# Fused top-k attention and mixture of experts: the first expert slot's gather goes ahead of its weights and one turn sooner

## The chip, the core and the metric

One NeuronCore of a Trainium2 chip runs the whole program. The metric is the device time of one execution in microseconds (us); the number given is the median of several executions. A profile is one execution of its own, with its own time.

## What is computed

The input is 8 batches of 8 heads with 576 positions of 64 numbers. Attention keeps, in every row of 576 scores, those that are at least the 32nd largest, and its output (4608 tokens of 512 numbers) goes through a mixture of 8 experts, of which each token uses one:

```python
scores = scale * np.matmul(q, k.transpose(0, 1, 3, 2))
kth = np.partition(scores, -32, axis=-1)[..., -32:-31]
attn = softmax(np.where(scores >= kth, scores, -1e9))
x = (attn @ v).transpose(0, 2, 1, 3).reshape(4608, 512)
logits = x @ w_gate + modality_bias[modality_id]
e_idx = np.argmax(logits, axis=1)
out[mask] = gate_w[mask, None] * (np.maximum(x[mask] @ w1[e], 0.0) @ w2[e])   # for each expert e
```

## The kernel before

The attention is cut into 288 tiles of 128 x 576 scores, 36 for a batch and 9 for a pair of heads. The main loop has one turn `i` for a tile, and every turn writes down one stage of some ten tiles: the scores of tile i+2 (`qk`, L384, copied to SBUF by ScalarE in `sevac`, L389), the search for the 32nd largest of tile i on VectorE (`subs`, `chain`, `find`, L396 to L438), the sign pass on ScalarE (`sign`, L428) and the product with it on GpSimd (`pool_y`, L434), the exponential, and the transposes of tile i-9 (`trans`, L492). `sign` of a turn writes one of two buffers K, so it waits for the `pool_y` of the turn before; `find` of a turn reads the y that the turn before wrote. In the first 48 tiles two of three use another path for the mask (`hide`, `hidden`, `masked`, L465 to L477), which gives GpSimd a second pass (L471).

When a batch is done its tokens are routed (`route`) and scattered by five indirect DMAs of GpSimd (`send`, L611) into a table `xs` in DRAM, sorted by expert. Expert work comes in slots of 256 rows of one expert. A slot picks its expert on VectorE (`sched`: `pick` and `done`, L677 to L693), reads the choice into a register of SyncE (`which`, L697), gathers its rows (`rows`, `xg<-xs`, L701), loads the expert's weights in four pieces each (`load_w1`, L722, and `load_w2`, L727), takes the token numbers (`tokens`, L713 to L716), turns the rows over on TensorE (`xt`, L769) and multiplies (`hid`, L796, and `outp`, L809). All these loads and the attention's own (`load`, L140 to L147, the V of a pair at the turns with j = 7) are issued by SyncE, in the order in which the program writes them.

What stands where is decided when the program is written, by lists and a ledger:

- `rush` holds the steps of a slot's start. A turn takes up to 18 of them and stops at a `PAUSE`, which it uses up. `sent` empties what is left of the scatters (`sends`); otherwise a turn sends two at its end. `go` lets the slot's products begin in the next turn.
- Weights wait in `wl`, from which a turn issues one piece at its end (none where j is 3 or 4); a product that needs a piece takes it out at once (`loaded`).
- The ledger `spare_pe` gains `STEP` = 3.4 a turn (1.0 from turn 294), loses the `COST` of the attention's products in this turn, gains 0.1 for each small step on VectorE and is capped at `CAP` = 2.6. As long as it is above zero, pieces of expert work are written into the turn: 0.22 for a quarter of `xt`, 0.88 for half an `hid` or one `outp`. After a block's last product the next block starts in the next turn at the earliest. Where no expert work is at hand, six bfloat16 products keep TensorE busy instead (`keep_warm`, L969).
- The main loop's last turn is 309. What is left of the expert work then follows, and six further slots are run one by one (`slot`, L1065 and L1081), after their rows and weights have been split in two parts by ScalarE and VectorE (`turn_rows`, L1036; `parts`, L1020 and L1021). `in_advance` writes the first of these splits among the leftovers.

The first slot starts at turn 50. Its list before the change is

```python
rush.extend(pick + [begin] + l1[:2] + done + [PAUSE, sent] + rows + [PAUSE, PAUSE] + go + [l1[2], l1[3], PAUSE] + tok)
```

where `pick` has ten entries, `done` five, and `l1` are the four pieces of w1.

Of the kernel before, what the change touches and what calls it, by code (L numbers as in the profile page):

```python
# [77 lines left out]
def kernel(  # L78
# [43 lines left out]
    PAUSE = lambda: None  # L122

    def load(p, what, b=None, queues={}):

        o = LD.setdefault(p, {})
        h0 = 2 * (p % HP)
        for nm in what:
            Q = queues.get(nm, SP)
            src = {"k": k, "q": q, "v": v}[nm]  # L130
            g = src[p // HP] if b is None else src[ds(b, 1)].rearrange("o h s d -> (o h) s d")
            if nm == "v":
                t = vtail[p % 2]
            else:
                if nm == "k":
                    o["kq"] = ld.tile([128, 2, D], FT, name="kqt", bufs=1)
                t = o["kq"][0:64] if nm == "k" else o["kq"][64:128]
            m = ld.tile([128, 2, 4, D] if nm == "v" else [128, 4, 2, D], FT, name=nm + "m", bufs=2 if nm == "v" else 1)
            if nm == "v":
                Q.dma_start(m.rearrange("p h c d -> p h (c d)"),  # L140
                             g[h0:h0 + 2, 0:512, :].rearrange("h (p c) d -> p h (c d)", c=4))
            else:
                for h in range(2):
                    Q.dma_start(m[:, :, h, :], g[h0 + h, 0:512, :].rearrange("(p c) d -> p c d", c=4))
            Q.dma_start(t[:64, 0:3:2, :] if nm == "v" else t, g[h0:h0 + 2, 512:, :].rearrange("h p d -> p h d"))
            if nm == "v":
                Q.dma_start(t[64:, 1, :], g[h0 + 1, 512:, :])  # L147
            o[nm] = (m, t)
# [496 lines left out]
    def chores():  # L645

        while chore:
            chore.popleft()()
# [76 lines left out]
    def load_w2(s, g):  # L725
        SL[s]["w2"][g] = True
        SP.dma_start(w2b[:, 2 * g:2 * g + 2, :],  # L727
                     w2[ds(SL[s]["e"], 1), g * 256:g * 256 + 256, :].rearrange("o (c p) d -> p (o c) d", p=128))
# [129 lines left out]
    rush = deque()  # L858
    moe = deque()
    sends = deque()  # L860
# [7 lines left out]
    def ready(n, whole):  # L868
# [5 lines left out]
        for g in range(4):  # L874
            load_w2(n, g)

    plan = {"ready": -1, "go": False}
    alone = [False]
    wl = deque()

    def weight(f):

        if alone[0]:
            f()
        else:
            wl.append(f)

    def more_moe():

        n = nslot[0]  # L890
        b = seen[0] // S
        full = PB[b - 1] if b <= len(PB) else int(seen[0] / SLOT - 0.9)
        fits = lambda x: x >= PB[-1]
        if plan["ready"] == n:
            if moe or not plan["go"]:
                return
            chores()
            nslot[0] += 1
            nxt = full >= n + 2
            moe.extend(expert(n, True, nxt, fits(n + 1), True))  # L900
            if nxt:
                plan.update(ready=n + 1, go=True)
        elif full >= n + 1:
            now = SL[n - 1] if moe else {"xt": True, "used": [4, 4]}
            if not now["xt"]:
                return
            plan.update(ready=n, go=False)
            pick, rows, done, tok = sched(n, fits(n))
            free = []

            def begin():
                free.extend(now["used"])
                now["nxt"] = True

            def take(x, g):
                return lambda: weight(lambda: (load_w1, load_w2)[x](n, g)) if g < free[x] else None
            l1 = [take(0, g) for g in range(4)]
            l2 = [f for g in range(4) for f in (take(1, g), PAUSE)]
            go = [lambda: plan.update(go=True)]
            if n == 0:  # L920
                def sent():

                    while sends:
                        sends.popleft()()
                rush.extend(pick + [begin] + l1[:2] + done + [PAUSE, sent] + rows + [PAUSE, PAUSE] + go + [l1[2], l1[3], PAUSE] + tok)
            else:
                begun, rest = ([], go) if moe else (go, [])
                rush.extend(pick + [begin] + rows + rest + l1[:1] + done + [PAUSE, l1[1], l1[2], PAUSE, l1[3]] + begun + [PAUSE] + tok)
            side.extend(l2)
# [189 lines left out]
    for i in range(LAST):  # L1119
# [5 lines left out]
        p, j = divmod(i, 9)  # L1125
# [49 lines left out]
        if p + 2 < NPAIR and j in LJ:  # L1175
            load(p + 2, "kq"[LJ.index(j)])
        if j == VJ and p < NPAIR:
            load(p, "v")
        b1, r = divmod(i - (TL + 1), 36)
        if b1 > SOON:  # L1180
            b1, r = divmod(i - (TL + 2), 36)
# [53 lines left out]
        while seen[0] and spare_pe > 0:  # L1235
            if i < NT + ME and not alone[0]:
                more_moe()
            if not moe:
                break
            c, f, new = moe[0]  # L1240
            if (new() if callable(new) else new) and after:
                break
            moe.popleft()
            f()
            spare_pe -= c
# [236 lines left out]
```

## Time and profile before

| | us |
|---|---|
| median of 3 executions | 1193.09 (1192.94 to 1196.3) |
| the profiled execution | 1193.59 |
| its span, first to last instruction | 1191.9 |
| TensorE busy (matmul) | 1153.1 |
| VectorE busy | 1093.2 |
| ScalarE busy | 983.2 |
| GpSimd busy | 675.8 |

PE is TensorE's matmul, PEld its weight load, DVE VectorE, ACT ScalarE, POOL GpSimd, SP SyncE; SPq and POOLq are the queues in which SyncE and GpSimd issue. The chain of work that ended last is followed back from the last instruction, at each step to what released it. A wait for several semaphores is put down to the one that came last. A busy share of 100% is not an engine at its peak: matmuls are pipelined and their ends modelled.

### The profile page before, as it was taken

The numbers are of one execution on the slowest core, as the hardware profiler recorded it, in microseconds if no ns is written. First come the engines' busy times: TensorE is split into PE (matmuls) and PEld (weight loads), VectorE is DVE, ScalarE is ACT, GpSimd is POOL, SyncE is SP. The second block draws the span as 40 slices with busy tenths as digits, with TensorE's granted clock in tenths as the row PEclk, the third lists the DMA queues.
The fourth block names the chain that finished last, engine by engine and source line by source line (L and its number), as shares of the span: only waits on it lengthen the run. The fifth ranks groups of instructions, "written<-read, shape, count | busy, mean of one in ns | idle before, by whom it ended". The sixth has DMA issues, their size and how long they took to land.

```text
span 1191.9 us, 28040 instructions
## 1 busy us (share of the span) xinstructions
PE 1153.1 (97%) x7908; PEld 904.7 (76%) x7908; DVE 1093.2 (92%) x5474; ACT 983.2 (82%) x2015; POOL 675.8 (57%) x1256
## 2 busy tenths in 40 slices
PE   8889979999999999999999999999999999999998
PEld 6766768778786868778687877778686877589987
DVE  7999999999999999999999999999999999476762
ACT  6999979998899989998899898889899888355652
POOL 6888885655656565556556566657555665221111
PEclk9999999999999999999999999999999999999999
DMA  5663367663576467664786458654765554287750
GB/s 128 167 173 89 89 168 208 186 168 97 158 229 175 121 169 207 168 168 128 205 238 172 111 144 239 170 155 133 198 197 129 155 167 139 69 286 246 248 193 22
DMA packets 204323, 197.09 MB, mean 165 GB/s; under 512 B 104413, under 2 KB 151533, under 8 KB 204160
## 3 DMA queue, kind: packets, MB, share of 16 engines
q1 hardware_dynamic: 196880, 175.92, 53.1%
q0 software_dynamic: 6080, 19.00, 4.4%
q8 instruction: 66, 1.08, 0.4%
q14 instruction: 97, 0.79, 0.2%
q10 hardware_dynamic: 1200, 0.30, 0.1%
HBM read 118.63 MB, written 24.23 MB: 120 GB/s over the span
## 4 chain that ended last, share of the span: by engine, by line
PE 61%; DVE 27%; ACT 6%; issue 2%; POOL 2%; DMA 1%; SPq 1%; POOLq 0%; ACTq 0%; DVEq 0%
PE E L809 12%; PE E L796 10%; PE X L520 9%; PE S L384 7%; DVE cand L396 7%; PE T L492 6%; PE X L1081 5%; DVE mg L438 4%; PE X L1065 4%; DVE P L458 4%; PE E L1065 1%; DVE cand L407 1%; ACT K L428 1%; DVE cand L408 1%; ACT Ssb L389 1%
## 5 line engine op out<-in xcount | busy, mean ns | idle before, releaser
L396 DVE MAX8 cand<-Ssb 128x8 f32<-128x96 f32 x1728 | 389.4, 245 | 2.0 <-ACT Ssb L389 2.0
L434 POOL TENSOR_TENSOR y<-Ssb,K 128x576 f32<-128x576 f32 x288 | 368.2, 1278 | 20.4 <-ACT K L428 19.6
L428 ACT ACTIVATE K<-Ssb,n 128x576 bf16<-128x576 f32 x288 | 229.6, 797 | 8.1 <-POOL y L434 7.4
L384 PE MATMUL S<-ks,qs 128*128 128x288 f32 x992 | 223.4, 347 | 11.2 <-ACT Ssb L389 7.0
L389 ACT ACTIVATE Ssb<-S 128x576 f32<-128x576 f32 x284 | 187.6, 661 | 52.4 <-PE S L384 31.9
L438 DVE MAX8 mg<-y 128x8 f32<-128x576 f32 x288 | 213.3, 741 | 1.9 <-POOL y L434 1.9
L796 PE MATMUL E<-xgT,w1b 128*128 128x256 f32 x832 | 201.0, 384 | 3.5 <-ACT hT L800 2.4
L452 ACT ACTIVATE ex<-Ssb,sm 128x576 f32<-128x576 f32 x256 | 202.4, 791 | 0.0
L384 PEld LDWEIGHTS S<-ks,qs 128*128 128x128 f32 x992 | 153.1, 191 | 59.5 <-issue 28.0
L500 ACT ACTIVATE PT<-T 128x640 f32<-128x640 f32 (+1 forms) x288 | 193.3, 671 | 5.9 <-PE T L492 5.7
L809 PE MATMUL E<-w2b,hT 128*128 128x512 f32 x416 | 195.4, 596 | 0.7 <-ACT hT L800 0.4
L458 DVE SCALAR_TENSOR_TENSOR P<-Ssb,kth,ex 128x576 f32<-128x576 f32 x230 | 191.9, 835 | 3.7 <-ACT ex L452 3.0
L492 PE MATMUL T<-idf,P 128*128 128x128 f32 x1152 | 169.5, 274 | 6.9 <-ACT P L477 5.6
L796 PEld LDWEIGHTS E<-xgT,w1b 128*128 128x128 f32 x832 | 150.9, 190 | 30.4 <-ACT hT L800 9.0
L481 POOL TENSOR_SCALAR spare<-P 1x1 f32<-1x1 f32 x230 | 42.6, 185 | 202.1 <-DVE mg L407 168.7
L492 PEld LDWEIGHTS T<-idf,P 128*128 128x128 f32 x1152 | 137.4, 140 | 12.9 <-ACT P L477 9.3
L520 PE MATMUL X<-PT,vm 128*64 128x256 f32 (+1 forms) x1536 | 145.1, 331 | 0.3
L421 POOL TENSOR_SCALAR n<-mg 128x1 f32<-128x1 f32 x288 | 69.8, 242 | 93.1 <-DVE mg L409 74.7
L520 PEld LDWEIGHTS X<-PT,vm 128*64 128x64 f32 x1536 | 87.8, 137 | 44.2 <-issue 10.9
L809 PEld LDWEIGHTS E<-w2b,hT 128*128 128x128 f32 x416 | 73.0, 190 | 60.2 <-issue 55.1
L1087 POOL DMA_INDIRECT out_dram<-ot,tk x12 | 12.3, 1023 | 91.2 <-ACT ot L1086 91.2
L428 ACT ACTIVATION_READ_ACCUMULATOR K<-Ssb,n 128x1 f32 x288 | 63.5, 221 | 0.0
(223 smaller groups left out, 2152.8 us busy)
## 6 DMA issues: line engine op xcount, KB each, us to landing
w1b<-in_moe_w_dram SPq DMA_DIRECT2D x76, 512.0 KB
w2b<-in_moe_w_dram SPq DMA_DIRECT2D x76, 512.0 KB
ks<-st SPq DMA_DIRECT2D x62, 288.0 KB
ks<-st SPq DMA_DIRECT2D x62, 256.0 KB
qs<-st SPq DMA_DIRECT2D x124, 128.0 KB
xg<-xs SPq DMA_DIRECT2D x19, 516.0 KB
vm<-in_v_dram SPq DMA_DIRECT2D x32, 256.0 KB
km<-in_k_dram SPq DMA_DIRECT2D x63, 128.0 KB
```

The costliest lines, as they stand in the source:

```text
L384: PE.matmul(ps[:, hf, :288], l, m, start=(n == 0), stop=(n == len(terms) - 1))
L389: A.activation(sb.rearrange("p (a b) -> p a b", a=2), T[i]["ps"], AF.Copy, scale=0.125)
L396: return [lambda s=s: V.max(c[:, s * 8:s * 8 + 8], T[i]["S"][:, bnd[s]:bnd[s + 1]]) for s in range(NSUB)]
L428: A.activation(t["K"], t["S"], AF.Sign, scale=2.0 ** -24 - 1.0, bias=t["n"][:, 1, i % 3:i % 3 + 1], accum_out=t["n"][:, 0, i % 3:i % 3 + 1])
L434: G.tensor_tensor(t["y"], t["S"], t["K"], op=OP.mult)
L438: V.max(t["mg"][:, i % 3, 24:32], t["y"])
L452: A.activation(t["ex"], t["S"], AF.Exp, bias=t["s"][:, i % 3:i % 3 + 1])
L458: V.scalar_tensor_tensor(t["P"], t["S"], kth[:, i:i + 1], t["ex"], op0=OP.is_ge, op1=OP.mult, accum_out=dn)
L492: PE.transpose(T[i]["pt"][:, x, :], (Pm if c == 4 else Pb[c % 2])[:, h * 512 + x * 128:h * 512 + x * 128 + 128], idf)
L520: PE.matmul(o.rearrange("p (a b) -> p a b", a=2) if j < 8 else o, l, r, start=(c == 0), stop=(c == 4))
L796: PE.matmul(ps[:, f % 2], w1b[:, c, f * 128:(f + 1) * 128], xgT[:, c, :], start=(c == 0), stop=(c == KC - 1))
L809: PE.matmul(o["py"], hT[:, f, t * 128:(t + 1) * 128], w2b[:, f, :], start=(f == 0), stop=(f == FC - 1))
```

## The change

The two first pieces of w1 move from ahead of the gather to behind it, one `PAUSE` behind the gather goes and one further down is added, and a load of V that falls due while scatters are still unsent is put on a list that is emptied behind `go`.

```diff
+    held_ = deque()
     plan = {"ready": -1, "go": False}
...
             if n == 0:
+                held = [lambda: [held_.popleft()() for _ in range(len(held_))]]
+
                 def sent():
 
                     while sends:
                         sends.popleft()()
-                rush.extend(pick + [begin] + l1[:2] + done + [PAUSE, sent] + rows + [PAUSE, PAUSE] + go + [l1[2], l1[3], PAUSE] + tok)
+                rush.extend(pick + [begin] + done + [PAUSE, sent] + rows + l1[:2] + [PAUSE] + go + held + [l1[2], l1[3], PAUSE, PAUSE] + tok)
...
         if j == VJ and p < NPAIR:
-            load(p, "v")
+            if sends:
+                held_.append(lambda p=p: load(p, "v"))
+            else:
+                load(p, "v")
```

## Rows read from the trace of the kernel before

**Rows 1.** The page's parts 1 and 4: busy time, and the chain by engine.

```profile
PE 1153.1 (97%) x7908; PEld 904.7 (76%) x7908; DVE 1093.2 (92%) x5474; ACT 983.2 (82%) x2015; POOL 675.8 (57%) x1256
...
PE 61%; DVE 27%; ACT 6%; issue 2%; POOL 2%; DMA 1%; SPq 1%; POOLq 0%; ACTq 0%; DVEq 0%
```

**Rows 2.** Chain of waits, 150 to 200 us: start, length, what.

```profile
165.22 1.27 POOL ex L471
...
172.44 1.24 POOL y L434
173.71 0.75 DVE mg L438
...
189.80 2.63 PE E L796 x12
```

**Rows 3.** Timeline of POOL: start, length, line, operation, count, [idle before, releaser].

```profile
167.89 1.02 POOL L611 DMA_INDIRECT xs<-x,dest  x1 [0.16 <-issue]
...
169.21 1.00 POOL L611 DMA_INDIRECT xs<-x,dest  x1 [0.20 <-issue]
...
170.85 0.94 POOL L611 DMA_INDIRECT xs<-x,dest  x1 [0.28 <-issue]
```

**Rows 4.** Timeline of DVE, the searches of turns 52 and 53.

```profile
169.41 0.74 DVE L438 MAX8 mg<-y 128x8 f32<-128x576 f32 x1
...
173.71 0.76 DVE L438 MAX8 mg<-y 128x8 f32<-128x576 f32 x1 [1.19 <-POOL y L434]
```

**Rows 5.** Timeline of ACT, the sign pass of turn 53.

```profile
173.71 0.77 ACT L428 ACTIVATE K<-Ssb,n 128x576 bf16<-128x576 f32 x1 [3.11 <-POOL y L434]
```

**Rows 6.** Timeline of PE, turns 53 to 55.

```profile
171.34 0.82 PE L969 MATMUL E<-onesb 128*128 128x256 bf16 x6
176.19 1.33 PE L384 MATMUL S<-ks,qs 128*128 128x288 f32 x4 [4.04 <-ACT Ssb L389]
...
178.87 1.49 PE L969 MATMUL E<-onesb 128*128 128x256 bf16 x6
...
185.56 0.66 PE L769 MATMUL E<-idf,xg 128*128 128x128 f32 x4
```

**Rows 7.** Windows of 2 us: length, busy by engine, granted clock, DMA share, GB/s.

```profile
174.00:176.00 2.00, 0.00 (x0) 0.00 (x0) 2.00 (x14) 1.75 (x4) 1.99 (x3) 0.84 0.84 296
176.00:178.00 2.00, 1.79 (x6) 1.44 (x7) 2.00 (x6) 2.00 (x5) 1.84 (x3) 0.50 0.05 15
...
182.00:184.00 2.00, 2.00 (x18) 1.42 (x19) 1.97 (x15) 2.00 (x6) 0.39 (x2) 0.96 0.49 173
```

**Rows 8.** Timeline of SP's queue, the loads around the first slot's gather.

```profile
169.52 0.46 SPq L722 DMA_DIRECT2D w1b<-in_moe_w_dram  x1
170.03 0.66 SPq L140 DMA_DIRECT2D vm<-in_v_dram  x1
...
177.13 0.36 SPq L701 DMA_DIRECT2D xg<-xs  x1
```

**Rows 9.** SP queue's waits, 160 to 180 us: total, times, longest.

```profile
SPq L701 <- DMA xs<-x,dest: 3.9, 1, 3.9
```

**Rows 10.** Chain of waits at a later slot's gather.

```profile
571.77 3.57 DMA xg<-xs
```

**Rows 11.** Chain of waits at the program's end, behind the last scatter but one.

```profile
1182.02 1.02 POOL out_dram L1087
...
1183.14 4.00 issue
```

**Rows 12.** Timeline of DVE: an instruction of turn 84, one of turn 90.

```profile
279.94 0.39 DVE L582 TENSOR_TENSOR lt<-X,rd 128x128 f32<-128x128 f32 x1 [2.56 <-PE X L574]
...
306.37 0.15 DVE L677 TENSOR_TENSOR s_av<-er 128x8 f32<-128x8 f32 x1
```

**Rows 13.** Timelines of PE and of DVE behind the main loop.

```profile
1038.99 6.28 PE L809 MATMUL E<-w2b,hT 128*128 128x512 f32 x14
...
1040.70 3.50 DVE L1021 TENSOR_TENSOR w1l<-w1b,w1h 128x1024 fp32r<-128x1024 f32 x3 [1.33 <-ACT w1h L1020]
```

## The prediction

> **What bounds the kernel now.** I read the busy times first: TensorE is busy 97% of the span and VectorE 92%, and the chain that ended last runs 61% over TensorE and 27% over VectorE [rows 1]. So most of the time follows TensorE, and a change at the first slot pays only where TensorE does without waiting, or what it need not do. Then the chain of waits about the slot: from 165.22 to 173.7 us it runs over GpSimd, then over VectorE, and at 189.80 it is on TensorE [rows 2]. The reason is in GpSimd's queue: two scatters end turn 51, the fifth opens turn 52, and each keeps GpSimd about 1.3 us from start to start [rows 3]. The products y of turn 52 come only at 172.44 [rows 2]; VectorE's search of turn 53 waits 1.19 us for them [rows 4], ScalarE's sign pass 3.11 us [rows 5], and behind that pass in ScalarE's queue stands the copy that frees the scores' PSUM, so TensorE waits 4.04 us, until 176.19 [rows 6]. Behind that hole TensorE runs at half its clock: granted 0.84 in the window that ends at 176, 0.50 after it, 0.96 in the one that starts at 182 [rows 7]. The gather is issued at 177.13, after 3.9 us of waiting for the scatters [rows 8, 9], and the slot's first transposes run at 185.56 [rows 6].
>
> **The order after the change.** The old list fills its 18 places with l1[:2], so the next turn is used up by the `PAUSE` alone, and the gather stands in turn 52. The new list has 16 steps and then the `PAUSE`: `sent` and the gather stand in turn 51, `go` in 52, the first transposes in 53 and not 55. `sent` finds three scatters unsent and writes them in one row, ahead of turn 51's y; at the top of turn 52 none is left, so V is loaded at its old place, behind the gather in SyncE's queue, and the new `held` list stays empty.
>
> **GpSimd and VectorE.** The three scatters begin at 166.65, after the pass of 165.22 [rows 2], and end near 170.3 (two starts 1.3 apart, and 1.0 for the last [rows 3]). Turn 51's y is then ready at 171.7 (1.3 more, and the gap of 0.16 ahead of it); it was there before 169.41, where VectorE's search of turn 52 starts without a wait [rows 4]. That search now waits 2.3 us; the wait of 1.19 in turn 53 goes, because y of turn 52 is no later than before (GpSimd's total is the same, in one turn fewer). VectorE: +1.1 us at turn 54.
>
> **SyncE and the gather.** Before, the fifth scatter's instruction ended at 171.79 [rows 3] and the gather went out at 177.13 [rows 8]: 5.3 us, beside w1 and V, which were issued at 169.52 and 170.03, just among them [rows 8]. Without them the nearest row is the program's end, where the release comes 4.0 us behind a scatter with the engines otherwise idle, though for 128 rows and not 64 [rows 11]. So the landing costs between something below 4.0 and 5.3; I take 4.0, since two pieces of w1 and a V, 1.3 MB, no longer run beside it: 170.3 + 4.0 = 174.3, 2.8 us earlier than now. The gather lands 3.57 us after its issue at another slot [rows 10]: 177.9. It is first in its queue, so the weights behind it don't delay it. Queued behind it are V and all four pieces of w1; some 2.4 MB (four pieces of 0.52 MB, and 0.3) at the 296 GB/s of a full window [rows 7] are in by 183, while V is needed just ahead of 185.56 [rows 6] and w1 at 189.80 [rows 2]. I cost them at nothing; if they came late, TensorE would stand in front of V, and that is in the range. On the price of a landing there is a rule that speaks against the change. The Trainium skill, page "DMA: Bandwidth & Descriptors", section "Anatomy of one DMA — SWDGE (gpsimd) path", puts a fixed 2.0 us on such a DMA, most of it the receipt from memory, plus its bytes at 436 GB/s: an estimate of 2.3 us for these 64 rows of 2 KB, whatever runs beside it. By it the gather would land at 176.2 and the sum below be about 1.7 us less; the 4.0 us of the program's end don't agree with it [rows 11], nor do the 5.3.
>
> **TensorE.** In turn 53 its products now end with two transposes that need the gather, and the scores of turn 54 stand behind them. From below it is ScalarE that holds these scores, as now, or a little sooner (175.9); from above it is a gather no faster behind its scatter than now (170.3 + 5.3 + 3.57 = 179.2, and 0.9 for the transposes at half clock). With 177.9 they start at 178.5: +2.3 us against 176.19 [rows 6]. The hole is now in two parts (about 169.9 to 173.1, where y of turn 51 is late, and 174.4 to 177.9), so I expect the half clock as now, and cost it at nothing more. Gone are two groups of warming products: 0.82 us that lay ahead of the hole and cost nothing, and 1.49 us at half clock in turn 54 [rows 6]: -1.5.
>
> **Expert work that moves.** Playing the ledger on from the constants: slot 0's first products move from turn 55 to 53, slot 1's from 75 to 72, slot 2's from 94 to 91 (its tokens are there from 90 on in either case); from turn 57 on the expert work is 3.5 units ahead, from about turn 96 to the end mostly 4.4, and of the 2.2 units left behind turn 309 none remains. A unit is one us: three pieces of 0.88 take 2.63 us [rows 2]. Where TensorE bounds, this only moves work: the early turns grow by what the late ones lose. It is worth something where VectorE bounds and TensorE has room. Turns 84 to 89 last 26.4 us from one early instruction of turn 84 to one of turn 90 [rows 12], and the ledger has 23.3 us of TensorE's work in them: 3.1 us of room, into which the new order puts 1.8 units more than the old one. -1.8.
>
> **The end.** Before, 14 records (7 pieces) of `outp`, 6.28 us, run while VectorE splits three pieces of w1 for 3.50 us, up to 1044.2 [rows 13]. The ledger leaves 5 pieces (4.4 us) behind the last transposes of x, so TensorE is through with them at 1042.9 (from 1038.5, half a us ahead of the row, which followed four transposes that are then no longer there) and with the slot's eight row transposes at 1043.9. VectorE is free at 1044.2 and needs 0.6 for half the rows (3.50/3 for 1024 columns, so half of it for 512): TensorE idles until 1044.8. +0.9; the bounds are 0 and 2, if rows or weights are later.
>
> **Sum.** +2.3 - 1.5 - 1.8 + 0.9 = -0.1 us on the execution of 1193.59 us; VectorE's +1.1 lies beside TensorE's +2.3. The profiled execution is 0.5 us above the median of the runs shown, so the forecast is 1193.0 us: the stall is not removed but moved, from ScalarE's queue to the gather.
>
> **Rivals.** *The gather holds TensorE (slower).* If scatters land no sooner after their issue than now, TensorE's turn 54 starts at 180.1: +3.9. The half clock, which lasted some 6 us behind the hole [rows 7], then covers 1.3 us of transposes and products that were not in these turns, which costs as much again, and VectorE is starved, so nothing is taken up later: +3.9 + 1.3 - 1.5 + 0.9 = +4.6, 1197.6 us. It decides from a landing at about 178.9 on. For it: the 5.3 us of now. Against it: the weights did run beside those scatters. To the same side belongs that later slots meet their gathers a turn earlier (slot 2's transposes one turn after its gather, and the chain already lost 3.57 us at one of them [rows 10]). *The hole closes (faster).* If the gather lands by 175.5, TensorE starts turn 54 at 175.9 (-0.3), has no hole of 4 us and keeps its clock, which gives back half of 6 us (-3.0); the warming products cost 0.82 and save that (-0.8), and with -1.8 and +0.9 this is -5.0, 1188.0 us. For it: DMA still moved 296 GB/s in the window up to 176 [rows 7], with w1 and V in it. Against it: y of turn 51 is late whatever the gather does, and TensorE is without scores until 173.1. *The weights were not what held the scatters, but nothing else hurts:* between forecast and first rival, and inside the forecast's band.
>
> **How the numbers follow.** A measurement of this kernel can tell about 0.3%, 3.6 us, from no change. The forecast has 0.58, with its own range 1189.6 to 1196.6 (no change); the gather that holds TensorE, with the later slots' gathers, 0.21 (slower); the closed hole 0.21 (faster). The range for 8 in 10 takes in both rivals' times: 1187.5 to 1198.0.
>
> **What would show it.** Three L611 in one row from 166.6; the search of turn 52 waiting about 2.3 us for y, and none in turn 53; the gather's issue near 174.3 with all w1b and V behind it; L769 twice, in turns 53 and 54, the first waiting for `xg`; 12 fewer records of L969; fewer `outp` behind the last transposes of x. The granted clock between 174 and 184 decides between forecast and faster rival, the start of turn 54's scores (175.9, 178.5 or 180.1) between all three. The prediction is wrong if the time follows neither: if VectorE bounds the whole attention, the 4.4 us of expert work moved early would be free, and the end would come 3 to 4 us sooner with the hole unchanged.

## The result, and the profile after

| | kernel before | changed kernel |
|---|---|---|
| median of 4 executions, us | 1193.28 (1192.94 to 1196.3) | 1208.76 (1206.77 to 1209.49) |
| ratio, 95% interval | | 1.0121 [1.0105, 1.0137] |
| the profiled execution, us | 1193.59 | 1206.77 |
| its span, us | 1191.9 | 1205.1 |

The changed kernel is 1.2% slower, outside the range of the prediction. The ratios in this text are not quotients of the medians (for the changed kernel the means give 1.0121, the medians 1.0130). From line 921 on, the lines of the changed kernel are three higher (L969 is L972, L1065 is L1068).

The page's parts 1 and 4, which answer [rows 1]:

```profile
PE 1155.7 (96%) x7896; PEld 907.4 (75%) x7896; DVE 1093.9 (91%) x5474; ACT 981.3 (81%) x2015; POOL 671.4 (56%) x1256
...
PE 68%; DVE 20%; ACT 6%; issue 2%; DMA 2%; SPq 1%; POOL 0%; POOLq 0%; ACTq 0%; DVEq 0%
```

The work is the same but for 12 products of `keep_warm`, and each engine's busy time is within 5 us of before. The 13 us are idle time and half clock. To see where they arise I take VectorE's search (L438), which stands once in every turn from 5 to 292, and subtract its start in the kernel before from its start in the changed one. This **lag** is -0.3 us at turn 51, 1.2 at turn 60, 1.8 at turn 107, 8.8 at turn 113, 9.75 at turn 292 (the last search), and 13.2 at the end of the span. So there are three steps: 1.6 us at the first slot, 7.0 at turns 107 to 113, 3.5 behind the last search. In between the lag goes up and down (it is 12.0 at turn 209), with 1.5 us left of it.

**The first slot.** Timelines of POOL, DVE, PE and SP's queue in the changed kernel (start, length, line, operation, count, [idle before, releaser]), for [rows 3, 4, 6, 8]:

```profile
166.31 1.01 POOL L611 DMA_INDIRECT xs<-x,dest  x1 [0.16 <-issue]
...
168.91 0.91 POOL L611 DMA_INDIRECT xs<-x,dest  x1 [0.22 <-issue]
...
169.88 1.28 POOL L434 TENSOR_TENSOR y<-Ssb,K 128x576 f32<-128x576 f32 x1
```
```profile
171.19 0.76 DVE L438 MAX8 mg<-y 128x8 f32<-128x576 f32 x1 [2.05 <-POOL y L434]
174.23 0.75 DVE L438 MAX8 mg<-y 128x8 f32<-128x576 f32 x1
```
```profile
172.64 1.33 PE L384 MATMUL S<-ks,qs 128*128 128x288 f32 x4 [3.10 <-ACT Ssb L389]
...
176.07 1.09 PE L769 MATMUL E<-idf,xg 128*128 128x128 f32 x4 [1.03 <-DMA xg<-xs]
...
177.66 1.31 PE L384 MATMUL S<-ks,qs 128*128 128x288 f32 x4
...
180.05 3.49 PE L796 MATMUL E<-xgT,w1b 128*128 128x256 f32 x12
```
```profile
171.99 0.38 SPq L701 DMA_DIRECT2D xg<-xs  x1
172.58 0.38 SPq L722 DMA_DIRECT2D w1b<-in_moe_w_dram  x1
```

Three scatters in a row, y behind them, one search that waits and the next that doesn't, the gather ahead of the weights, the transposes held by it, the scores of the turn behind them at 177.66: the forecast order is all there. Windows of PE's clock, where 0.50 is the lower of its two levels, for [rows 7] (length, busy by engine, granted clock, DMA share, GB/s):

```profile
170.00:172.00 2.00, 0.00 (x0) 0.00 (x0) 0.81 (x3) 0.81 (x3) 1.84 (x4) 0.82 0.59 209
172.00:174.00 2.00, 1.36 (x6) 1.35 (x7) 2.00 (x15) 2.00 (x6) 1.31 (x3) 0.50 0.44 136
...
178.00:180.00 2.00, 2.00 (x11) 1.98 (x10) 1.93 (x10) 1.97 (x5) 0.71 (x1) 0.50 0.36 119
180.00:182.00 2.00, 2.00 (x8) 1.68 (x7) 1.97 (x11) 1.40 (x3) 1.92 (x3) 0.62 0.78 259
```

**The large step.** PE and SP's queue at 360 us, and the chain of waits there (start, length, what):

```profile
354.44 1.88 PE L809 MATMUL E<-w2b,hT 128*128 128x512 f32 x4
...
360.70 1.02 PE L809 MATMUL E<-w2b,hT 128*128 128x512 f32 x2
367.12 3.78 PE L809 MATMUL E<-w2b,hT 128*128 128x512 f32 x4 [5.39 <-DMA w2b<-in_moe_w_dram]
```
```profile
336.01 0.43 SPq L727 DMA_DIRECT2D w2b<-in_moe_w_dram  x1
336.69 1.87 SPq L722 DMA_DIRECT2D w1b<-in_moe_w_dram  x2
338.77 0.94 SPq L727 DMA_DIRECT2D w2b<-in_moe_w_dram  x2
...
359.69 0.43 SPq L722 DMA_DIRECT2D w1b<-in_moe_w_dram  x1
...
362.34 0.43 SPq L727 DMA_DIRECT2D w2b<-in_moe_w_dram  x1
```
```profile
362.34 4.74 DMA w2b<-in_moe_w_dram
```

An x4 here is four records of `outp`; two records make a product. The fourth piece of slot 2's w2 is issued at 362.34, 0.6 us after TensorE has run out of work, and lands 4.74 us later. Four records then take 3.78 us, with a granted clock of 0.59 from 365 to 370 us; at full clock four take 1.88 (the row of 354.44). Between the third piece (in the row of 338.77) and the fourth stand 23 us, and in front of the fourth a piece of w1 that belongs to slot 3 (359.69). In the kernel before all four left together, and slot 3's first piece followed:

```profile
333.94 2.93 SPq L727 DMA_DIRECT2D w2b<-in_moe_w_dram  x4
...
338.31 0.37 SPq L722 DMA_DIRECT2D w1b<-in_moe_w_dram  x1
```

The program's own order says why. Slot 2 starts at turn 91, not 94, and so slot 3's gather and its first w1 pieces are written sooner (the gather in turn 96, not 101); but slot 2's w2 pieces enter the list `wl` at the pace of `side`, the queue of small steps from which a turn takes a few. So two pieces of slot 3's w1 get in line ahead of three of slot 2's w2, and a third ahead of the last. A turn issues one piece, and none where j is 3 or 4 (turns 102 and 103). The last piece is taken out in turn 105, the turn that uses it; before, it left eight turns ahead of its use.

**The end.** PE and ACT behind the main loop, for [rows 13]:

```profile
1046.12 0.18 PE L602 MATMUL X<-ohb,tri 128*128 128x40 bf16 x1 [1.37 <-DVE x L554]
...
1050.76 4.46 PE L809 MATMUL E<-w2b,hT 128*128 128x512 f32 x10
...
1057.47 0.35 PE L1068 MATMUL X<-xgh,w1h 128*128 128x256 f32 x1 [1.38 <-POOL spare L537]
1058.88 0.58 PE L1068 MATMUL X<-xgl,w1h 128*128 128x256 f32 x1 [1.05 <-DVE xgl L1024]
1059.25 0.42 PE L1068 MATMUL X<-xgh,w1l 128*128 128x256 f32 x1
```
```profile
1047.13 2.00 ACT L1023 ACTIVATE w1h<-w1b 128x1024 fp32r<-128x1024 f32 x2
1055.25 0.69 ACT L819 ACTIVATE ot<-E,sgt 128x512 f32<-128x512 f32 x1 [6.12 <-PE E L809]
1055.84 1.05 ACT L1023 ACTIVATE w1h<-w1b 128x1024 fp32r<-128x1024 f32 x1
```

Ten records of `outp` (five products) stand behind the last transposes of x, as forecast; before there were sixteen (eight). But with fewer pieces left `in_advance` has written only two splits of w1 ahead of the last result copy (L819), not three. The third split stands behind that copy in ScalarE's queue (1055.84 behind 1055.25), and the copy waits 6.12 us for its products; the split of the rows comes behind both, at 1056.78. TensorE waits 1.38 and 1.05 us for those splits (the profile names a memset of GpSimd for the first wait; that ScalarE's split of the rows, which ends about then, is what it waits for is read off, not tested). It waits 1.37 earlier, for VectorE's copy of x (L554), where the kernel before runs one product of `outp` (1032.54, 1.02 us long) and waits 0.27. Then it runs at half clock (granted 0.50 from 1060 to 1062 us) for some 15 records (0.42 us long; 0.28 later on).

The lag is VectorE's, and at the last search it hides part of TensorE's: TensorE starts the last logits (L565) at 1038.67 against 1027.06, 11.6 us behind and not 9.75. So 1.9 of the 3.5 us are products that TensorE had done ahead and that VectorE's row doesn't show yet (in e5 below, where that lead is handed back at turn 286, the two lags agree within 0.1). By the starts of TensorE's later rows in both kernels, the wait at L602 adds 0.7, the way to the first row of L1068 gives back 1.3 (fewer products, less the wait of 1.38), the second wait adds 0.7 and the half clock 1.4.

### The profile page after: what moved, and what is told of

Read it like the earlier page. It is cut to its first block, busy times and chain, and to the rows that moved or that the text cites. A ratio compares the mean times of both kernels' runs of the same rounds, so it can differ in the third digit from the quotient of the medians.

```text
span 1205.1 us, 28021 instructions
## 1 busy us (share of the span) xinstructions
PE 1155.7 (96%) x7896; PEld 907.4 (75%) x7896; DVE 1093.9 (91%) x5474; ACT 981.3 (81%) x2015; POOL 671.4 (56%) x1256
## 4 chain that ended last, share of the span: by engine, by line
PE 68%; DVE 20%; ACT 6%; issue 2%; DMA 2%; SPq 1%; POOL 0%; POOLq 0%; ACTq 0%; DVEq 0%
PE E L796 13%; PE E L809 12%; PE X L520 11%; PE S L384 9%; PE T L492 7%; DVE cand L396 5%; PE X L1084 5%; PE X L1068 4%; DVE mg L438 3%; DVE P L458 3%; PE E L1068 1%; PE X L318 1%; ACT Ssb L389 1%; ACT K L428 1%; DVE hT L465 1%
## 5 line engine op out<-in xcount | busy, mean ns | idle before, releaser
L438 DVE MAX8 mg<-y 128x8 f32<-128x576 f32 x288 | 213.1, 740 | 2.7 <-POOL y L434 2.7
L809 PE MATMUL E<-w2b,hT 128*128 128x512 f32 x416 | 196.9, 601 | 5.7 <-DMA w2b<-in_moe_w_dram 5.4
L809 PEld LDWEIGHTS E<-w2b,hT 128*128 128x128 f32 x416 | 73.6, 191 | 67.7 <-issue 57.4
```

Source lines behind the costliest of these rows:

```text
L438: V.max(t["mg"][:, i % 3, 24:32], t["y"])
L809: PE.matmul(o["py"], hT[:, f, t * 128:(t + 1) * 128], w2b[:, f, :], start=(f == 0), stop=(f == FC - 1))
```

## The experiments

The theory at this point: the first slot itself is nearly free, and the loss comes from the expert work that runs three to four products ahead from then on, through one piece of w2 and through the end. Rival 1 puts it down to the new order of scatters and loads; rival 2 says that work ahead of its loads must wait somewhere, so that the piece is only where it shows first. The lags (us behind the kernel before's profiled execution, start of L438; the end is the span's):

| run | median, us | ratio, 95% interval | turn 51 | 60 | 107 | 113 | 292 | end |
|---|---|---|---|---|---|---|---|---|
| changed | 1208.76 | 1.0121 [1.0105, 1.0137] | -0.3 | 1.2 | 1.8 | 8.8 | 9.75 | 13.2 |
| e1_go_late | 1195.72 | 1.0015 [1.0004, 1.0026] | 0.9 | 1.3 | 0.6 | 0.6 | 2.1 | 2.0 |
| e2_go_early | 1212.62 | 1.0157 [1.0139, 1.0175] | 0.1 | 1.1 | 4.4 | 12.6 | 15.8 | 19.3 |
| e3_w2_ahead | 1199.68 | 1.0050 [1.0034, 1.0067] | 0.25 | 1.8 | 1.8 | 1.5 | 2.2 | 5.7 |
| e4_late_w2 | 1200.03 | 1.0060 [1.0040, 1.0080] | 0.1 | 0.1 | 0.0 | 4.9 | 4.6 | 4.5 |
| e5_hold_last | 1196.77 | 1.0017 [1.0006, 1.0028] | 0.4 | 2.0 | 1.45 | 1.1 | 1.85 | 1.8 |
| e6_less_left | 1200.99 | 1.0042 [1.0020, 1.0063] | 0.65 | 0.6 | -0.1 | -0.1 | 2.3 | 7.5 |
| e7_one_turn | 1199.13 | 1.0037 [1.0022, 1.0051] | -0.2 | 0.9 | 2.1 | 2.1 | 4.85 | 4.7 |
| e8_spread | 1193.91 | 0.9994 [0.9981, 1.0008] | -0.2 | -0.4 | -0.5 | -0.4 | -0.5 | -0.5 |

The kernel before had 1193.16 us beside e1 to e4 and 1194.45 beside e5 to e8. Turn 51 lies ahead of every change, so its column is what an execution brings along from its start; where the text says so, it is taken off.

### The first slot without the lead, and the lead without the first slot's order

```diff
-... + done + [PAUSE, sent] + rows + l1[:2] + [PAUSE] + go + held + [l1[2], l1[3], PAUSE, PAUSE] + tok)
+... + done + [PAUSE, sent] + rows + l1[:2] + [PAUSE, PAUSE, PAUSE] + go + held + [l1[2], l1[3], PAUSE] + tok)
```

> The changed kernel with two more PAUSEs ahead of go: the gather ahead of the weights and the three scatters in one row stay, but the first slot's products start at turn 55 as before, so every later load and product has the turn it had before the change. Theory (the first slot itself costs nothing, and the 13 us come from the expert work that runs three to four products ahead later on): no wait at outp of slot 2, the end as before, and a total of 1191 to 1195 us. Rival 1 (the bunched scatters and the loads queued behind the gather cost the time, there and in what follows): at least half of the loss stays, 1200 us or more.

Measured: 1195.72 us, 0.7 above the theory's range and far from the rival's 1200. All later products and loads have their old turns, and there is no step at turn 107 and none at the end. Of the lag of 2.0 at the end, 0.9 was there at the start, and at turn 113 it is 0.6; the rest comes in near turn 185 (see Open). TensorE doesn't meet the gather, and its windows show half clock for some 3 us only:

```profile
174.00:176.00 2.00, 2.00 (x9) 1.98 (x10) 2.00 (x11) 1.74 (x4) 1.07 (x4) 0.50 0.94 317
176.00:178.00 2.00, 1.95 (x11) 1.25 (x10) 2.00 (x14) 1.18 (x3) 2.00 (x2) 0.69 1.10 369
178.00:180.00 2.00, 1.46 (x13) 1.18 (x12) 2.00 (x12) 2.00 (x6) 1.84 (x4) 1.00 1.10 360
```

The other half of the pair is the kernel before with a `PAUSE` less:

```diff
-... + l1[:2] + done + [PAUSE, sent] + rows + [PAUSE, PAUSE] + go + [l1[2], l1[3], PAUSE] + tok)
+... + l1[:2] + done + [PAUSE, sent] + rows + [PAUSE] + go + [l1[2], l1[3], PAUSE, PAUSE] + tok)
```

> The kernel before with one PAUSE fewer ahead of go: w1 and V stay among the scatters and the gather stays in turn 52, but from slot 1 on every load and product has the turn that it has in the changed kernel, the last w2 piece of slot 2 among them, loaded in its turn of use. Theory: TensorE waits some 5 us for that piece near 360 us, the end is as in the changed kernel, and the total is 1204 to 1210 us. Rival 1 (the new order of scatters and loads costs the time): 1192 to 1197 us, since that order isn't there.

Measured: 1212.62 us, more than both expected. The old order with the new lead is slower than the changed kernel, so the new order isn't what costs. Its waits of PE (total, times, longest):

```profile
PE E L809 <- DMA w2b<-in_moe_w_dram: 5.7, 1, 5.7
PE X L781 <- DMA xg<-xs: 3.4, 2, 1.9
PE E L769 <- DMA xg<-xs: 2.6, 2, 1.9
```

The same wait for w2, the same 3.5 us at the end, and some 6 us more than the changed kernel: 2.3 up to turn 84 (start taken off; TensorE waits 1.9 us for the first gather, and slot 1 starts at turn 72), 1.2 in the step itself, which is 8.2 here, and most of the rest in turns 218 to 221. Rival 1 falls by both runs.

### The late piece alone, taken away and added

```diff
         if wl and j not in HOLD:
-            wl.popleft()()
+            for _ in range(3 if i == 101 else 1):
+                wl.popleft()()
```

> The changed kernel with one edit at turn 101: three pieces leave the waiting list of weights there and not one, so that the last w2 piece of slot 2 goes out four turns ahead of its use (105), and one w1 piece of slot 3 three turns sooner than it did. Theory: the wait of 5.4 us at outp and the half clock behind it go, the lag behind the kernel before stays near 1.8 us through turn 110 (it rose to 8.8), and the total falls by 6 to 7.5 us, to 1201 to 1203 us. Rival 2 (expert work that runs ahead starves TensorE of weights or rows anyway, and this piece is only where it shows first): another wait takes its place within the next turns, and the total stays above 1206 us.

Measured: 1199.68 us, 9 us less than the changed kernel in the median and 7.5 in the profiled spans (5.7 against 13.2). The lag goes from 1.8 at turn 107 to 1.5 at 113, where it had gone to 8.8, and nothing takes its place up to turn 292 (in between it goes up to 4.4 and comes back, by the same 3 us as in the changed kernel). PE at that point:

```profile
360.89 2.74 PE L809 MATMUL E<-w2b,hT 128*128 128x512 f32 x6
...
366.80 2.74 PE L809 MATMUL E<-w2b,hT 128*128 128x512 f32 x6
```

So rival 2 falls. The same piece made late in the kernel before, without any lead:

```diff
-            if o["nxt"]:
+            if o["nxt"] and not (s == 1 and x == 1 and o["used"][x] == 4):
...
         def loaded(what, g):
+            if defer and s == 2 and what == "w2" and g == 3 and g not in o[what]:
+                load_w2(2, 3)
             while defer and g not in o[what]:
```

> The kernel before, in which the last w2 piece of slot 2 is loaded in its turn of use (107) and not at turn 99; nothing else of its order changes but that two w1 pieces of slot 3 go one or a few turns sooner. Theory: one load at its use costs what it costs in the changed kernel, 5 us of wait and 1 to 2 of half clock: 1198.5 to 1201 us. Rival 2 (the wait alone is hidden by VectorE's work, and costs only where expert work runs ahead): 1193 to 1196 us.

Measured: 1200.03 us, 6.9 above the kernel before. In the profile it is one step of 4.9 us, and it stays to the end (4.5):

```profile
369.18 2.85 PE L811 MATMUL E<-w2b,hT 128*128 128x512 f32 x4 [3.18 <-DMA w2b<-in_moe_w_dram]
```

The wait is 2.2 us shorter than in the changed kernel: here the piece is issued at 364.30, 1.7 us before TensorE runs out of work, there 0.6 us after. One load in the turn of its use costs 5 to 8 us, with or without expert work ahead: 4.9 in this profile and 6.9 in this median (the profiled execution, 1198.15 us, is this run's fastest), 7.0 in the changed kernel and 8.2 in e2.

### The end alone, taken away and added

```diff
-            if moe or not plan["go"]:
+            if moe or not plan["go"] or n == 12 and i < 286:
                 return
```

> The kernel of e3_w2_ahead, in which slot 12 may not start ahead of turn 286. So it runs three to four products ahead up to turn 285, and from 286 on every product has the turn it had in the kernel before: seven are left behind the main loop and not two. Theory (the 3.5 us that the runs with a lead lose between the last search of turn 288 and the end come from the missing leftovers, which fill TensorE while the last batch is routed): the end costs what it cost before, and the total is 1195 to 1197.5 us. Rival (the lead is repaid wherever it ends, since the products held back only come later): it stays at 1199 to 1200.5 us.

Measured: 1196.77 us, 2.9 less than e3, and 4.2 less when each is taken against the kernel before beside it (2.3 above it, e3 6.5). Behind turn 292 nothing is lost (1.85 to 1.8), and PE's rows are again those of [rows 13], followed by the slot's products without a wait:

```profile
1040.76 6.28 PE L809 MATMUL E<-w2b,hT 128*128 128x512 f32 x14
...
1048.20 0.68 PE L1068 MATMUL X<-xgh,w1h 128*128 128x256 f32 x1
```

And the kernel before with four more products in turn 285:

```diff
         spare_pe = min(spare_pe + (STEP if i < NT + TL + END[0] else END[1]) - cost, CAP)
+        spare_pe += 1.2 * (284 <= i < 286)
```

> The kernel before with four products of slot 12 more in turn 285 (the ledger gains 1.2 in turns 284 and 285), so that from turn 286 on every product has the turn it has in the changed kernel and two, not seven, are left behind the main loop; nothing ahead of turn 284 changes. Theory: the end alone costs what it cost the changed kernel, 3 to 4 us: 1195.5 to 1198 us. Rival (what is done ahead is saved behind): 1192 to 1194.5 us.

Measured: 1200.99 us, above the theory's 1195.5 to 1198; the rival's gain is not there at all. The lag rises from 1.2 at turn 287 to 2.3 at 292, which fits the four products more in turn 285, and then by 5.2, not 3.5. The holes are the changed kernel's to a hundredth, but one stretch of half clock is added (L809, four records in 3.08 us):

```profile
1038.68 0.18 PE L602 MATMUL X<-ohb,tri 128*128 128x40 bf16 x1 [1.36 <-DVE x L554]
...
1039.86 3.08 PE L809 MATMUL E<-w2b,hT 128*128 128x512 f32 x4
...
1051.71 0.36 PE L1065 MATMUL X<-xgh,w1h 128*128 128x256 f32 x1 [1.38 <-POOL spare L537]
1053.12 0.39 PE L1065 MATMUL X<-xgl,w1h 128*128 128x256 f32 x1 [1.05 <-DVE xgl L1021]
```

Over all runs: where five products stand behind the last transposes of x, the end loses 3.5, 3.5, 3.5 and 5.2 us (changed, e2, e3, e6); where eight stand there, between -0.2 and 0 (e1, e4, e5, e7, e8). The seven and two of the expectations count the entries of the list `moe` at the end of turn 307, not products, and not what is left behind turn 309.

### What the first slot's 1.6 us are

In e7 `go` of e5 is one turn later (`[PAUSE, PAUSE] + go` for `[PAUSE] + go`).

> The kernel of e5_hold_last with go one turn later, so that the first transposes of slot 0 stand in turn 54, not 53; slot 1 starts at turn 72 in both. Theory (the first slot cost 1.6 us at turn 55 because TensorE met the gather in turn 53, waited 1.03 us for it and stayed at half clock until 181 us): no wait for the gather, full clock by 178 us, a lag near 0.5 us at turn 60, and 1 us less than e5 in all, 1194 to 1196.5 us. Rival (that lag is the expert work done ahead, which must be paid at some turn): no difference to e5.

Measured: 1199.13 us, 2.4 more than e5, so this theory falls, and the rival's "no difference" with it. TensorE no longer waits for the gather and has its full clock sooner (at 178.5 us, in e5 at 179.6), as expected, but the lag at turn 60 is 1.1 us (start taken off) against e5's 1.6, and then 1.3 are added in turns 68 and 76 and 1.4 in turns 218 to 221. The first, which e2 shows too, fits that slot 0 has a turn less for the same products up to slot 1's start (argued, not tested); the second, which e2 has too and e5 hasn't, goes with a second wait for a later gather (L781: 3.5 us in two waits, in e5 1.6 in one). Why that gather is met only in these two runs is open. In e8 the scatters are not brought together:

```diff
-... + done + [PAUSE, sent] + rows + l1[:2] + [PAUSE] + go + held + [l1[2], l1[3], PAUSE, PAUSE] + tok)
+... + done + [PAUSE, PAUSE, PAUSE, sent] + rows + l1[:2] + held + [PAUSE] + go + [l1[2], l1[3], PAUSE] + tok)
```

> The new order of loads, but the three scatters are not brought together: two leave at the end of turn 51, the last at the end of turn 52, behind y of that turn, and the gather is in turn 53; go stays where it was in the kernel before, so all later work has the turn it had there. Theory (the hole at 172 us stands where a product y waits behind scatters in GpSimd's queue): y of turn 52 comes 1.3 us sooner than in the kernel before, the hole of 4.04 us shrinks to 2.7 or less, half clock for no longer than 3 us, and the total is 1190 to 1193 us. Rival (GpSimd has too much to do in these turns whatever the order; the delay moves to turn 53, or TensorE meets the later gather in turn 55): 1193 to 1196 us.

Measured: 1193.91 us, no change. y of turn 52 does come 1.8 us sooner (170.60, for [rows 2]), and yet the hole stays. POOL, ACT and PE of e8:

```profile
172.03 0.95 POOL L611 DMA_INDIRECT xs<-x,dest  x1 [0.16 <-issue]
...
173.78 1.27 POOL L471 TENSOR_TENSOR ex<-Ssb,hT 128x576 f32<-128x576 f32 x1
```
```profile
175.08 0.65 ACT L389 ACTIVATE Ssb<-S 128x576 f32<-128x576 f32 x1 [1.64 <-POOL ex L471]
```
```profile
175.78 1.33 PE L384 MATMUL S<-ks,qs 128*128 128x288 f32 x4 [3.82 <-ACT Ssb L389]
```

The copy that TensorE waits for now waits for GpSimd's second pass, which stands behind the scatter in GpSimd's queue. The rival is right: in these turns GpSimd has five scatters, a y in each turn and a second pass in most, and each of the three orders tried only chooses who waits.

## Why the prediction was wrong, by its steps

**Right.** The order at the first slot; the search of turn 52 waiting (2.05 us, forecast 2.3), the next one not; TensorE meeting the gather in turn 53; 12 records of L972 fewer; five pieces behind the last transposes of x.

**Mis-sized.** The landing of the scatters: 171.99 - 169.82 (the end of the last one) = 2.2 us, where I took 4.0 from [rows 11]. I misread that row. Its 4.00 us are "issue", not a landing, and the engines were not idle: the scatter behind it waits for a result copy of ScalarE, which ends at 1187.1 and waits for TensorE's products, which run until 1186.3. ACT and POOL of the kernel before:

```profile
1186.41 0.69 ACT L1086 ACTIVATE ot<-E,gt 128x512 f32<-128x512 f32 x1 [4.66 <-PEq L1445]
```
```profile
1187.37 0.98 POOL L1087 DMA_INDIRECT out_dram<-ot,tk  x1 [4.23 <-ACT ot L1086]
```

The estimate of 2.3 us that I had worked out from the Trainium skill, page "DMA: Bandwidth & Descriptors", section "Anatomy of one DMA — SWDGE (gpsimd) path", agrees with the 2.2, and my objection from [rows 11] to it falls. That it holds whatever runs beside the scatter is not borne out: it took 5.3 and 5.8 us where w1 and V were issued among the scatters (last section). Two other sizes took back 1.5 of the 2.3 us by which the gather goes out ahead of the forecast (171.99, not 174.3). The transposes start 4.1 us after the gather's issue (171.99 to 176.07), not 3.57, and take 1.6 us to the scores of turn 54 (176.07 to 177.66), where my sum had 0.6; so those scores start at 177.66, not 178.5.

The half clock lasts some 10 us in the changed kernel's profile (171.3 to 181.5, read from the granted clock of the windows), which looks like a miss of "as now". It isn't one: e3 and e5 have the same program up to turn 100 and a second wait of 1.5 and 0.9 us for the gather, and there it lasts 6.8 us (174.8 to 181.7 and 172.8 to 179.6), as before the change. The lag at turn 60, start taken off, is 1.6 us in all three, so the longer stretch is not what it consists of. What it does consist of, beside the lead (e1, without it, has 0.4), no run here separates. The forecast was 0.8.

The room of turns 84 to 89: the lag falls by 0.6 us in them, not by 1.8. The end: 3.5 us, not 0.9. My sum took TensorE as having caught up with its early products by then (1.9 us were still to be paid) and the splits as running as early as before; with fewer leftovers there are fewer places to write them, and they queue behind the last result copy. "The bounds are 0 and 2" left out ScalarE's queue. With these sizes the terms of my sum make 1.6 - 0.6 + 3.5 = 4.5 us; 7.0 of the 13.5 (start taken off) had no term at all, and 2.0 are the ups and downs.

**The step that failed.** "Where TensorE bounds, this only moves work." I followed the products of slots 1 to 12 to their new turns and gave their loads no line of their own, although the ledger's order held both. "I cost them at nothing" was worked out for slot 0's w1 and V alone. Slot 2 went three turns sooner; its last w2 piece went six turns later (105, not 99), into the turn of its use. That is 7.0 us in the profile, and it was no rival: the first one named later gathers, but not the weights. Those gathers cost 2.9 us of waits at two slots (1.3 of the first row and 1.6 of the second, waits of PE in the changed kernel: total, times, longest; the kernel before has one such wait, of 0.7 us), part of the ups and downs between turns 60 and 292:

```profile
PE E L769 <- DMA xg<-xs: 2.4, 2, 1.3
...
PE X L781 <- DMA xg<-xs: 1.6, 1, 1.6
```

Undoing the piece (e3) gives back 7.5 to 9 us, undoing the end as well (e5) 2.9 to 4.2 more, and what then remains, 1.4 us with the start taken off, lies inside the forecast's band.

**The faster rival.** The hole doesn't close by an early gather: it was there in every order tried, 4.0 us in the old one, 3.1 with the scatters in one row and 3.8 with them spread.

**Open.** The lag of some runs rises by 1 to 2 us near turn 185 and partly comes back; e1 and e6 do so too (by 1.6 and 0.8 us in turns 182 to 185, and there most of it stays), which have the turns of the kernel before there, and e4 and e8 don't; so a step of this size in one profiled execution is no sign of a kernel. Why the changed kernel's median lies 2 us above its profiled execution wasn't looked into. No version tried beats the kernel before; e8 equals it.

## What to carry to other kernels

When a change starts a block sooner, write down for every later block the turn in which each load goes out beside the turn that first needs it: the products moved by three turns, the loads went through another list with its own pace, and one of the 104 pieces of slots 0 to 12 lost its whole margin. A load in the turn of its use costs its landing, its queue and the half clock behind the hole, here 5 to 8 us. And work left over at the end of a phase may be the cover of the next one: taking it away in advance saved nothing here, since the engines' queues then waited on each other.

## What the runs showed of the hardware

From the end of the last scatter's instruction to the gather's issue it took 5.3 us in the kernel before and 5.8 in e2, where w1 and V are issued among the scatters, and 2.2, 1.8, 2.1, 2.4, 2.1 and 1.7 in the changed kernel, e1, e3, e5, e7 and e8, where they aren't. So the new order does what the change is for; I had not expected that the other loads make up more than half of it. That it is these loads is read from the two groups of runs; no run moves them alone. A w2 piece of 512 KB took 4.74 us from issue to landing at 362 us, and 4.83 in e4 at 364; what of it TensorE has no other work for is waiting time (5.39 and 3.18 us).
